# Fewer and wider constant matmuls, one filter couple moved to VectorE, and the last pair's loads and reflections reordered

## The chip, the core and the metric

The kernel runs on one core of one Trainium2 chip. The metric is the device time of an execution in microseconds, lower is better. Engines carry the profile's names: PE (matmuls) and PEld (its weight loads), DVE (VectorE), ACT (ScalarE), POOL (GpSimd) and SP (SyncE, which only issues DMAs here).

## The reference

Two operations follow each other. The first is a causal long convolution along the sequence, done by FFT at double length. The second transforms its output along the sequence, mixes the lowest 64 modes with complex 128 x 128 weights, adds the inverse transform, and ends in a rectified linear layer.

```
x: (8, 5696, 128)   h: (5696, 128)   L = 2 * 5696
x1 = irfft(rfft(x, n=L, axis=1) * rfft(h, n=L, axis=0), n=L, axis=1)[:, :5696]
X = rfft(x1, axis=1)
Y = 0;  Y[:, :64] = einsum('bmd,mde->bme', X[:, :64], w_r + i w_i)
u = x1 + irfft(Y, n=5696, axis=1)
out = u + max(u @ w_ch, 0)          (float32)
```

## The kernel before

All transforms are matmuls with constant matrices in fp16. The sequence is cut as 5696 = 89 x 64. The frequencies of the first cut are k = 0 to 89 (`NK` = 90) and are taken four at a time, which makes 23 ticks (`NT`). The eight batches go in four pairs (`NP`).

The stages, in order:

1. **Start.** `idle(WARM, 6)` issues 52 matmuls of constants into two unused PSUM banks. They compute nothing that is read. Meanwhile h, the constant matrix `M` and the first pair's x (eight pieces `Xr`) are loaded by POOL's queue, and DVE and ACT copy h into the padded tile `Hp`.
2. **h transform.** 64 matmuls make `Ah` from `Hp`.
3. **Filter stage.** Twelve filter couples (`filter_couple`), each for two ticks: 32 matmuls of 64 columns (8 in the last couple) into one of three pairs of PSUM banks, then one cast to `Hs`. Couples 1 and 3 are cast by DVE, the others by ACT. After each couple stand two constant matmuls. After couple 4 is recorded, DVE gets two copies inside `M` (`m_cross`) and then the eight copies `x_place` of `Xr` into the padded tile `Xin`. Four constant matmuls end the stage. SP copies pieces of `Hs` between the halves of the partitions; these copies also wait for the last piece of `Xr`.
4. **a_tiles.** 32 tiles of four matmuls each make `As` from `Xin`. Every a_tile reads all of `Xin`. ACT and DVE share the casts. Then come four constant matmuls.
5. **Ticks of a pair.** `second` (matmuls with `M`), `products` (the multiplication with `Hs` on DVE, after an ACT copy in three ticks of four), `third` (matmuls with `Wc`, cast by ACT, stored to `zscr` by SP), and `modes_of` (matmuls with `G` that collect the 64 modes in PSUM). The next pair's x is loaded and placed meanwhile. At the end of pairs 0 to 2 the next pair's a_tiles follow, and four constant matmuls behind them.
6. **After the last pair.** Two casts give the modes `XT`, the second of them on DVE; `mix` multiplies the modes with the weights `W`, eight transposes and two casts give `C`. The first Z products (`u_z`, tiles `ZT` loaded back from `zscr`, matrix `S4`) are interleaved by hand.
7. **Output.** Z products and `C` products (matrix `IBs`) make `UT`, and a last matmul, a rectifier on ACT and a sum on DVE make the output.

`S4` and `IBs` are loaded only in their first half. The second half is that half reversed and multiplied by a sign per row (`reflect`: DVE for `S4a` and `IBs`, ACT for `S4b`).

The order on every engine is that in which the source records the instructions; nothing is rescheduled. The recorder derives the semaphores from readers and writers of named tokens; an engine stops at the first instruction whose tokens are not there. In the last pair the loads for the output stage are spread over ticks by the table `early`; each entry's loads and clears wait for that tick's product (`pace`). `ZT0`, `ZT1` and so on are five buffers in two parts, of 128 rows (a) and of 52 rows (b) with a cleared margin (`clear_zt`, a memset on POOL); they lie over `As`, `Hs` and `M`, and so each can be loaded only when the ticks that read what lies there are done.

Of the kernel before, what the change touches and what calls it, by code (L numbers as in the profile page):

```python
# [4 lines left out]
P = 128  # L5
# [118 lines left out]
def bass_long_conv_fft__then__afno_spectral_mix_kernel(nc, x, h, moe_w_r, moe_w_i, moe_w_ch, out):  # L124
# [7 lines left out]
    NK = NQ + 1  # L132
    NP = B // 2
# [27 lines left out]
    RB, PB = 2 * NK - P, 32  # L161
# [130 lines left out]
    def ap(t, row, p0, n, off, dims):  # L292
        return bass.AP(t, p0 * row + off, [[row, n]] + [list(d) for d in dims])
# [5 lines left out]
    def pv(bank, off, dims, p0=0, n=P):  # L299
        return bass.AP(ps, p0 * 4096 + bank * 512 + off, [[4096, n]] + [list(d) for d in dims])  # L300
# [10 lines left out]
    def evac(dst, src, reads, writes, scale=None, eng=None, after=()):  # L311
        e = eng
        if e is None:
            turn[0] ^= 1
            e = "scalar" if turn[0] else "vector"
        if e == "scalar":
            if scale is None:
                R.add(e, lambda h_: h_.copy(dst, src), reads, writes, after=after)  # L318
            else:
                R.add(e, lambda h_: h_.activation(dst, src, COPY, scale=scale), reads, writes, after=after)  # L320
        elif scale is None:
            R.add(e, lambda h_: h_.tensor_copy(dst, src), reads, writes, after=after)  # L322
        else:
            R.add(e, lambda h_: h_.tensor_scalar_mul(dst, src, scale), reads, writes, after=after)  # L324
# [4 lines left out]
    def mm(o, l, r, st, sp, reads, writes):  # L329
        R.add("tensor", lambda h_: h_.matmul(o, l, r, start=st, stop=sp), reads, writes)  # L330
# [11 lines left out]
    def turns(name, items):  # L342
        i = ring2.get(name, 0)
        ring2[name] = i + 1
        return items[i % len(items)]
# [24 lines left out]
    def x_place(i, src, toks):  # L370
        R.add("vector", lambda e: e.tensor_copy(bass.AP(x_sb, i * XN * XE, [[XW, NQ], [XE, XN], [XQ, 4], [1, XD]]),
                                                bass.AP(src, 0, [[XB, NQ], [D, XN], [XD, 4], [1, XD]])),
              list(toks) + XZ, [("xin", i)])
# [40 lines left out]
    XSLOT = [0, 2]  # L414
    ZBANK = [4, 5, 6]
    MB = 7
    WARM = 52


    def idle(n, b0, m=P):  # L420
        for i in range(n):
            mm(pv(b0 + i % 2, 0, [[2 * NK, 2], [1, 2 * NK]], 0, m), f1_sb[:, 0:m], ap(f1_sb, 2 * NK, 0, P, 0, [[0, 2], [1, 2 * NK]]),
               True, True, [("f1",)], [bank(b0 + i % 2)])

    idle(WARM, 6)
# [54 lines left out]
    def filter_couple(c_, sl, eng):  # L480
        ks = [k for t in (2 * c_, 2 * c_ + 1) if t < NT for k in ticks[t]]
        n = len(ks)
        for i, k in enumerate(ks):
            for r in range(2):
                for c in range(2):
                    mm(pv(sl + c, i * H2, [[1, H2]]), ap(m_sb, MW, J * c, J, m_col(c, k, r), [[1, P]]),
                       ap(ah_sb, HW, J * c, J, (2 * k + r) * H2, [[1, H2]]), r == 0, r == 1,
                       AHT + mtok(k, c) + [("ag", k)], [bank(sl + c)])
        lo, t1 = ks[0] * D, min(2 * c_ + 1, NT - 1)
        hi = lo + n * D  # L490
        evac(bass.AP(h_sb, lo, [[2 * HW, P], [H2, 2], [D, n], [1, H2]]), pv(sl, 0, [[512, 2], [H2, n], [1, H2]]), [bank(sl), bank(sl + 1)],
             [("h", t, 0) for t in range(2 * c_, t1 + 1)], eng=eng)
        if t1 in HEND:
            g0 = ([-1] + HEND)[HEND.index(t1)] + 1
            lo = KT * g0 * D
            for p0, p1 in ((0, J), (J, 0)):
                dma("sync", h_sb[p0:p0 + J, HW + lo:HW + hi], h_sb[p1:p1 + J, lo:hi], "s", XR[-1] + [("h", i, 0) for i in range(g0, t1 + 1)],
                    [("h", i, 1, p0) for i in range(g0, t1 + 1)])
# [22 lines left out]
    ZX = [("zs", i, b) for i in range(NZ, NZL) for b in range(2)]  # L521
    zt_old = [(AST, AST), (AST, AST), (H_ALL, H_ALL), (H_ALL, H_ALL), (M_ALL[6:12], G_ALL)]

    def load_zt(i, eng="sync", more=()):
        g_, c_ = divmod(i, J // ZB)
        for part, (p0, r0, n) in enumerate(((0, 0, P), (PB, P, RB))):
            old = list(once(("zt", i % NC, part), zt_old[i % NC][part])) + list(more) + pace
            dma(eng, bass.AP(zt[i % NC][part], p0 * ZP, [[ZP, n], [1, ZP]]),
                bass.AP(zs, (g_ * 2 * NK + r0) * J * 256 + c_ * ZB * 256, [[J * 256, n], [1, ZP]]),
                "q" if eng == "gpsimd" else "t", [("zd", g_, s_) for s_ in range(NT)], [("zt", i % NC, part)], after=old)  # L530

    def clear_zt(i):
        z32 = zt[i][1][0:PB, :].bitcast(U32)
        R.add("gpsimd", lambda e: e.memset(z32, 0), (), [("zt0", i)], after=list(zt_old[i][1]) + pace)

    def load_ib():
        dma("gpsimd", ib_sb[:, 0:SH], c_ib.ap(), "p", (), [("ib", 0)], after=M_ALL[0:4] + pace)
# [10 lines left out]
    def load_s4(part):  # L548
        n = PB + RB if part else P
        dma("gpsimd", s4_sb[part][0:n, 0:SH], bass.AP(c_s4, part * SH, [[2 * SH, n], [1, SH]]), "p", (),  # L550
            [("s4", part, 0)], after=pace + (AST if part else M_ALL[2:8]))

    V, A = "vector", "scalar"
    early = {0: lambda: (load_w(6), load_w(7), load_id()),
             6: lambda: load_s4(1), 8: lambda: load_ib(), 10: lambda: load_zt(2, "gpsimd"), 11: lambda: clear_zt(2),
             14: lambda: clear_zt(0), 15: lambda: load_zt(0, "gpsimd"), 16: lambda: load_s4(0),
             NT - 2: lambda: (load_zt(1, "gpsimd", SLACK), clear_zt(1))}
    w_at = {11: (0, 1), 17: (2, 3), 25: (4, 5)}
    pace = []
# [128 lines left out]
    SLOTS = [0, 2, 4, 6]  # L688
    NH = (NT + 1) // 2
    for c_ in range(NH):  # L690
        filter_couple(c_, turns("f", SLOTS[0:3]), "vector" if c_ in (1, 3) else "scalar")
        idle(2, 6)
        if c_ == 4:
            m_cross(4, "vector")
            m_cross(5, "vector")
            for i in range(2 * XC):
                x_place(i, x_raw[i], XR[i])
    idle(4, 6)
    load.update(scalar=0.0, vector=0.0)
    for j in range(32):  # L700
        a_tile(j, [turns("s", SLOTS)], "both" if j == 31 else share(720))
    idle(4, turns("s", SLOTS))
    for g_ in range(NP):
        for t in range(NT + LM if g_ + 1 == NP else NT):
            if g_ == 0 and t % 2 == 0 and t // 2 < NG:
                load_g(t // 2)
            tick(g_, t)
            assert g_ + 1 < NP or not wp
            if g_ == NP - 1 and t in early:
                pace[:] = [("u", min(t, NT - 1) % NU)] if t else []  # L710
                early[t]()
        if g_ + 1 < NP:
            load.update(scalar=600.0, vector=0.0)
            third(g_, NT - 2)
            a_tile(0, [0], share(720))
            a_tile(1, [2], share(720))
            third(g_, NT - 1)
            load["scalar"] += 560.0
            a_tile(2, [0], share(720))
            modes_of(g_, NT - 3)  # L720
            a_tile(3, [4], share(720))
            modes_of(g_, NT - 2)
            a_tile(4, [2], share(720))
            modes_of(g_, NT - 1)
            load["scalar"] += 700.0
        evac(bass.AP(xt, 6 * g_ + 2, [[B * XTW, P], [3 * B, M], [2, 2], [1, 2]]), pv(MB, 0, [[1, M], [M, 2], [P, 2]]),
             [bank(MB)], [("xt", g_)], 1.0 / 64, eng="scalar", after=[("ag", k) for k in range(NS + 2 * XN, NK)])
        evac(bass.AP(xt, 6 * g_, [[B * XTW, P], [3 * B, M], [1, 2]]), pv(MB, M, [[1, M], [P, 2]]),
             [bank(MB)], [("xtn", g_)], -1.0 / 64, eng="vector" if g_ + 1 == NP else "scalar", after=[("ag", k) for k in range(NS + 2 * XN, NK)])
        if g_ + 1 < NP:  # L730
            for j in range(5, 32):
                a_tile(j, [(0, 4, 6, 2)[(j - 5) % 4]], "both" if j == 31 else share(720))
                if j == 31:
                    idle(4, 2)
                if wp and j % 2 == 1:
                    dst, src_, ring, tok = wp.pop(0)
                    dma("gpsimd", dst, src_, ring, (), [tok], after=[("as", j)])
                if g_ + 2 == NP:
                    for i in w_at.get(j, ()):
                        load_w(i)  # L740
# [54 lines left out]
             src, [bank(t), bank(t + 1)], [("u_", ub, 2 * c_ + half)], eng=e, after=once(("u", ub), old))  # L795

    XTT = [(n, g_) for g_ in range(NP) for n in ("xt", "xtn")]
    reflect("vector", s4_sb[0], P, 0, ("s4", 0), M_ALL[2:8])
    reflect("scalar", s4_sb[1], PB + RB, 1, ("s4", 1), AST)
    MQ = M // 4  # L800

# [25 lines left out]
    for hb in range(2):  # L827
        evac(c_sb[:, hb * 512:hb * 512 + 512], ps16[:, (6 + hb) * 1024:(6 + hb) * 1024 + 512], [bank(6 + hb)],
             [("c", hb)], 2.0 * 64 / S, eng="vector" if hb else "scalar", after=WT)
    reflect("vector", ib_sb, P, 2, ("ib",), M_ALL[0:6])  # L830


    n_o = [0]
# [101 lines left out]
```

## Time and profile before

| | us |
|---|---|
| median of 3 runs | 378.26 (377.53 to 379.01) |
| the profiled execution | 377.14 |
| its span, first to last instruction | 375.3 |

Mean granted clock of the profiled execution: 0.998 of full speed.

The stages in the trace, in us from the start of the span:

| stage | from | to |
|---|---|---|
| constants at the start | 2.5 | 13.4 |
| h transform | 13.5 | 20.9 |
| filter stage | 20.9 | 35.8 |
| a_tiles of the first pair | 35.8 | 49.3 |
| last pair's ticks | 212.4 | 253.1 |
| mode products, `C` | 253.1 | 260.5 |
| output | 260.5 | 375.3 |

In the lines of the timeline the columns are: start, length, engine, source line, operation, output <- input, number of instructions that are merged in the line, and in brackets the engine's idle time before it and what ended that. In the chain of waits they are: start, length, and the engine or transfer that the chain runs through. Line 330 is the helper that issues every matmul, line 327 the one that issues every DMA, and lines 318 to 324 are the casts of `evac`; so the tiles tell the stages apart. The tile `F` is `f1_sb`: a matmul `ps<-F` is one of the constants.

### The profile page before, as it was taken

Reading aid. Unit: us, or ns where it says so; the run is one execution under the profiler, and the core shown is the slowest. Engines: PE = TensorE matmul, PEld = TensorE weight load, DVE = VectorE, ACT = ScalarE, POOL = GpSimd, SP = SyncE. Lnnn points to the kernel's source line nnn. Section 1 sums busy time; section 2 is a strip of 40 time slices with the busy share of each in tenths; the row PEclk is TensorE's granted clock in tenths of the full one; section 3 lists DMA queues with packets and bytes.
Section 4 is the critical chain, followed back from the end, with each engine's and each line's share of the span. In section 5 each row is a group of like instructions: output and inputs, shape, how many; then the busy total and the mean of one; then the engine's idle time right before and its main releaser. Section 6 shows DMA issues by size and latency. Waiting matters only on the chain.

```text
span 375.3 us, 12160 instructions
## 1 busy us (share of the span) xinstructions
PE 354.7 (95%) x5208; PEld 267.0 (71%) x5208; DVE 300.7 (80%) x333; ACT 313.4 (84%) x494; POOL 92.0 (25%) x138
## 2 busy tenths in 40 slices
PE   7987989999989999999999899999999999999992
PEld 3755856667856667766667666668898988888871
DVE  7675998998989998889998888764357776787784
ACT  8766989998989998999998899995466777777783
POOL 8760012320923311822213403427000000000000
PEclk9999999999999999999999999999999999999999
DMA  8995939998999996999998989999999999999767
GB/s 140 314 210 132 231 97 239 275 267 244 108 137 220 257 264 170 138 146 228 219 247 193 294 303 294 312 351 372 393 392 391 392 414 416 407 402 359 303 272 298
DMA packets 84129, 101.71 MB, mean 271 GB/s; under 512 B 22078, under 2 KB 68926, under 8 KB 81106
## 3 DMA queue, kind: packets, MB, share of 16 engines
q1 hardware_dynamic: 59643, 67.73, 53.0%
q0 software_dynamic: 24432, 33.20, 43.3%
q8 instruction: 41, 0.67, 0.7%
q14 instruction: 13, 0.11, 0.1%
HBM read 68.38 MB, written 51.12 MB: 318 GB/s over the span
## 4 chain that ended last, share of the span: by engine, by line
PE 79%; ACT 10%; DVE 5%; DMA 3%; issue 2%; DVEq 0%; POOL 0%; POOLq 0%
PE ps L330 79%; ACT As L320 7%; DMA Hin<-in_h_dram 3%; DVE As L324 2%; ACT R L869 1%; DVE U L616 1%; ACT UT L318 1%; ACT Hp L440 1%; DVE Ah L324 0%; DVE UT L322 0%; ACT Ah L320 0%; ACT XT L320 0%; DVE O L870 0%; DVE Os L870 0%; DVEq L105 0%
## 5 line engine op out<-in xcount | busy, mean ns | idle before, releaser
L330 PE MATMUL ps<-U,Wc 128*128 128x512 f16 (+1 forms) x368 | 94.4, 376 | 0.0
L624 DVE TENSOR_TENSOR U<-Xs,Hs 128x2048 f16<-128x2048 f16 (+1 forms) x68 | 80.6, 1188 | 10.9 <-ACT Xs L318 8.8
L318 ACT CAST Xs<-ps 128x1024 f16<-128x1024 f32 (+1 forms) x72 | 69.5, 971 | 7.1 <-PE ps L330 4.9
L870 DVE TENSOR_TENSOR O<-ps,R 128x512 f32<-128x512 f32 x81 | 52.5, 685 | 19.6 <-ACT R L869 12.3
L318 ACT CAST Zs<-ps 128x512 f16<-128x512 f32 (+1 forms) x120 | 62.9, 603 | 0.0
L869 ACT ACTIVATE R<-ps 128x512 f32<-128x512 f32 x96 | 50.9, 572 | 14.3 <-PE ps L330 13.9
L324 DVE TENSOR_SCALAR As<-ps 128x720 f16<-128x720 f32 (+1 forms) x63 | 51.9, 879 | 8.1 <-PE ps L330 7.0
L330 PE MATMUL ps<-As,M 64*128 64x128 f16 x1440 | 48.7, 217 | 4.6 <-DVE U L616 3.5
L330 PE MATMUL ps<-F,Xin 128*128 128x180 f16 x512 | 51.5, 247 | 1.5 <-DVE As L324 0.8
L320 ACT ACTIVATE As<-ps 128x720 f16<-128x720 f32 (+1 forms) x69 | 48.6, 765 | 5.0 <-PE ps L330 4.2
L330 PE MATMUL ps<-WI,UT 128*128 128x256 f16 x360 | 51.8, 279 | 0.5 <-DVE O L870 0.4
L330 PEld LDWEIGHTS ps<-F,Xin 128*128 128x128 f16 x512 | 43.2, 141 | 9.6 <-DVE As L324 5.0
L330 PEld LDWEIGHTS ps<-U,Wc 128*128 128x128 f16 x368 | 28.2, 97 | 28.9 <-ACT Zs L318 6.0
L330 PEld LDWEIGHTS ps<-As,M 64*128 64x128 f16 x1440 | 40.3, 94 | 11.2 <-DVE U L616 4.2
L327 POOL DMA_DIRECT2D Xt<-in_x_dram x48 | 24.8, 520 | 89.6 <-PE ps L330 89.0
L624 DVE TENSOR_TENSOR U<-ps,Hs 128x2048 f16<-128x2048 f32 x20 | 45.7, 2284 | 0.0
L318 ACT CAST UT<-ps 128x712 f16<-128x712 f32 x40 | 30.0, 752 | 16.7 <-PE ps L330 15.8
L330 PEld LDWEIGHTS ps<-WI,UT 128*128 128x128 f16 x360 | 39.3, 152 | 4.2 <-issue 1.9
L330 PE MATMUL ps<-IBs,C 128*128 128x356 f16 x128 | 39.2, 314 | 0.8
L330 PEld LDWEIGHTS ps<-G,Zs 128*128 128x128 f16 x468 | 25.7, 96 | 12.0
L318 ACT CAST Zt<-ps 128x512 f16<-128x512 f32 (+1 forms) x64 | 33.8, 604 | 0.1
L330 PE MATMUL ps<-G,Zs 128*128 128x2 f16 (+2 forms) x468 | 28.8, 191 | 0.0
(91 smaller groups left out, 495.4 us busy)
## 6 DMA issues: line engine op xcount, KB each, us to landing
out_dram<-O SPq DMA_DIRECT2D x39, 512.0 KB, 7.4
zscr<-Zs SPq DMA_DIRECT2D x57, 256.0 KB, 6.9
zscr<-Zt SPq DMA_DIRECT2D x31, 256.0 KB, 7.6
Xt<-in_x_dram POOLq DMA_DIRECT2D x24, 320.0 KB, 6.8
W<-wscr POOLq DMA_DIRECT2D x8, 512.0 KB, 10.4
ZT0a<-zscr SPq DMA_DIRECT2D x3, 1024.0 KB, 9.6
Xr<-in_x_dram POOLq DMA_DIRECT2D x8, 320.0 KB, 17.5
M<-cM POOLq DMA_DIRECT2D x3, 720.0 KB, 12.5
```

The costliest lines, as they stand in the source:

```text
L318: R.add(e, lambda h_: h_.copy(dst, src), reads, writes, after=after)
L320: R.add(e, lambda h_: h_.activation(dst, src, COPY, scale=scale), reads, writes, after=after)
L324: R.add(e, lambda h_: h_.tensor_scalar_mul(dst, src, scale), reads, writes, after=after)
L327: R.add(eng, lambda h_: h_.dma_start(dst, src), reads, writes, ring=ring, after=after)
L330: R.add("tensor", lambda h_: h_.matmul(o, l, r, start=st, stop=sp), reads, writes)
L440: R.add("scalar", lambda e, dst=dst, src=src: e.copy(dst, src), HT, [("hp", c_)])
L616: R.add("vector", lambda e, b=b, s_=s_: e.tensor_tensor(bass.AP(u_s[i], b * 512, [[2048, P], [1024, 2], [1, n * D]]), s_, hv, MULT), [tok, ...
L624: R.add("vector", lambda e: e.tensor_tensor(uv, src, hv, MULT), bk + [("h", t, 0), ("h", t, 1, 0), ("h", t, 1, J)], [("u", i)])
L869: R.add("scalar", lambda e: e.activation(rv, src_r, RELU), bk, [("r", i % NR)], after=once(("r", i % NR), G_ALL + XTT + [("y", q) for q in ...
L870: R.add("vector", lambda e: e.tensor_tensor(ov, src_u, rv, ADD), bk + [("r", i % NR)], [key + (h_,)], after=once(key, old))
```

## The change

- `idle` issues matmuls of 512 columns instead of 360. At the start 37 instead of 52; after each filter couple one instead of two; at the end of the filter stage two instead of four; after the a_tiles of each pair three instead of four. In all 63 instead of 96.
- Filter couple 9 is cast by DVE instead of ACT. It stands in DVE's queue between the seventh and the eighth `x_place`; the eighth is recorded after the loop over the couples.
- In the last pair `ZT2` and `ZT0` are loaded in two parts each, at ticks 9 and 12 and at ticks 10 and 14 instead of at 10 and at 15; `ZT2`'s clear moves from tick 11 to 10.
- The reflections of `IBs` and `S4a` on DVE stand ahead of the casts to `XT` of the last pair, instead of behind them and behind the casts to `C`.

```diff
-    WARM = 52
-    def idle(n, b0, m=P):
+    WARM = 37
+    def idle(n, b0):
         for i in range(n):
-            mm(pv(b0 + i % 2, 0, [[2 * NK, 2], [1, 2 * NK]], 0, m), f1_sb[:, 0:m], ap(f1_sb, 2 * NK, 0, P, 0, [[0, 2], [1, 2 * NK]]),
+            mm(pv(b0 + i % 2, 0, [[1, 512]]), f1_sb[:, 0:P], ap(f1_sb, 2 * NK, 0, P, 0, [[0, 4], [1, P]]),
                True, True, [("f1",)], [bank(b0 + i % 2)])
...
-    def load_zt(i, eng="sync", more=()):
+    def load_zt(i, eng="sync", more=(), parts=(0, 1)):
         g_, c_ = divmod(i, J // ZB)
-        for part, (p0, r0, n) in enumerate(((0, 0, P), (PB, P, RB))):
+        for part in parts:
+            p0, r0, n = ((0, 0, P), (PB, P, RB))[part]
...
-             6: lambda: load_s4(1), 8: lambda: load_ib(), 10: lambda: load_zt(2, "gpsimd"), 11: lambda: clear_zt(2),
-             14: lambda: clear_zt(0), 15: lambda: load_zt(0, "gpsimd"), 16: lambda: load_s4(0),
+             6: lambda: load_s4(1), 8: lambda: load_ib(), 9: lambda: load_zt(2, "gpsimd", (), (0,)),
+             10: lambda: (clear_zt(2), load_zt(0, "gpsimd", (), (0,))), 12: lambda: load_zt(2, "gpsimd", (), (1,)),
+             14: lambda: (clear_zt(0), load_zt(0, "gpsimd", (), (1,))), 16: lambda: load_s4(0),
...
-        filter_couple(c_, turns("f", SLOTS[0:3]), "vector" if c_ in (1, 3) else "scalar")
-        idle(2, 6)
+        filter_couple(c_, turns("f", SLOTS[0:3]), "vector" if c_ in (1, 3, 9) else "scalar")
+        idle(1, 6)
         if c_ == 4:
             m_cross(4, "vector")
             m_cross(5, "vector")
-            for i in range(2 * XC):
+            for i in range(2 * XC - 1):
                 x_place(i, x_raw[i], XR[i])
-    idle(4, 6)
+    x_place(2 * XC - 1, x_raw[-1], XR[-1])
+    idle(2, 6)
...
-    idle(4, turns("s", SLOTS))
+    idle(3, turns("s", SLOTS))
...
+        if g_ + 1 == NP:
+            reflect("vector", ib_sb, P, 2, ("ib",), M_ALL[0:6])
+            reflect("vector", s4_sb[0], P, 0, ("s4", 0), M_ALL[2:8])
         evac(bass.AP(xt, 6 * g_ + 2, ...            (the two casts to XT)
...
-                    idle(4, 2)
+                    idle(3, 2)
...
-    reflect("vector", s4_sb[0], P, 0, ("s4", 0), M_ALL[2:8])
...
-    reflect("vector", ib_sb, P, 2, ("ib",), M_ALL[0:6])
```

## The prediction

> **What bounds the kernel now.** I read the page first (busy shares, DMA queues), then the chain of waits in order of time, then the timeline of the stages that the change touches. The profiled execution took 377.14 us, 1.84 more than its span.
>
> ```profile
> span 375.3 us, 12160 instructions
> PE 354.7 (95%) x5208; PEld 267.0 (71%) x5208; DVE 300.7 (80%) x333; ACT 313.4 (84%) x494; POOL 92.0 (25%) x138
> q8 instruction: 41, 0.67, 0.7%
> ```
>
> PE has work almost throughout, so a gain must come from a place where PE stands still or does needless work on the path. The constant matmuls that the change shortens lie mostly in the first 50 us. The chain there:
>
> ```profile
> 20.89 6.54 PE ps L330 x235
> 27.43 1.51 issue
> 28.94 4.01 PE ps L330 x128
> 32.96 1.08 issue
> 34.04 13.83 PE ps L330 x149
> ```
>
> Two pauses stand in it that no engine or transfer ends ("issue"), 1.51 and 1.08 us, and between them lie exactly 128 matmuls. A matmul has a weight load, so that is 256 instructions. PE has 5208 of each, 10416 instructions, and the instruction queue moved 41 packets: one packet to about 254 instructions, 0.67 MB / 41 = 16 KB each. I read the pauses as PE at the end of an instruction block whose successor has not arrived, at a time when the loads of x fill the DMA queues. From one pause's end to the next it takes 34.04 - 28.94 = 5.10 us. So while these loads run, a block costs about 5.1 us, however fast PE eats its 128 matmuls.
>
> The rest of the filter stage (start us, duration, engine, line, operation):
>
> ```profile
> 23.84 0.64 PE L330 MATMUL ps<-Ah,M 64*128 64x64 f16 x32
> 24.41 0.48 PE L330 MATMUL ps<-F 128*128 128x360 f16 x2
> 24.52 1.23 DVE L322 CAST Hs<-ps 128x1024 f16<-128x1024 f32 x1 [0.74 <-PE ps L330]
> 24.82 0.64 PE L330 MATMUL ps<-Ah,M 64*128 64x64 f16 x32
> ...
> 27.65 4.38 DVE L371 COPY Xin<-Xr 89x2048 f16<-89x2048 f16 x7
> ...
> 29.18 3.97 ACT L318 CAST Hs<-ps 128x1024 f16<-128x1024 f32 x4 [1.68 <-PE ps L330]
> ...
> 33.20 0.69 DVE L371 COPY Xin<-Xr 89x2048 f16<-89x2048 f16 x1 [1.17 <-DMA Xr<-in_x_dram]
> ...
> 34.92 1.09 PE L330 MATMUL ps<-F 128*128 128x360 f16 x6
> ```
> ```profile
> 35.85 12.51 PE L330 MATMUL ps<-F,Xin 128*128 128x180 f16 x128
> ```
>
> The first a_tile needs all eight x_place copies. The last of them ends at 33.20 + 0.69 = 33.89, but PE begins its first a_tile only at 35.85, because it still has couples 10 and 11 and six constant matmuls to do after the second pause. These 1.96 us are what is to be had here.
>
> **Filter stage.** A couple takes 24.82 - 23.84 = 0.98 us: 0.57 for 32 matmuls, then 0.41 for two constants. Six constants took 1.09 us; with 0.32 for the last one's full duration (row below), they start (1.09 - 0.32) / 5 = 0.155 apart, and 512 columns at that rate make 0.22. One such in place of two saves 0.09: a couple takes 0.89, unless a block is late.
>
> Where the blocks end moves. Ahead of the pause at 27.43 PE has had 52 + 64 + 6 x 34 + 31 = 351 matmuls. With 37 at the start and 33 per couple, matmul 352 is the 20th of couple 7 (37 + 64 + 7 x 33 = 332), and the next block begins 128 on, at the fifth matmul of the a_tiles. The block before was entered at couple 3's sixth matmul, 23.94; now it is at couple 3's 24th, 20.89 + 3 x 0.89 + 0.41 = 23.97. So the block arrives as before, at about 29.0, but PE is a couple further on when it stops (27.5). After it: 13 matmuls (0.23) and the constant (0.22 + 0.10 to the next couple) to 29.55, couples 8 to 11 at 29.55, 30.44, 31.33, 32.22, and with the last eight matmuls and three constants PE is ready at 33.1. The next block, 5.10 us after 29.0, is there at 34.1.
>
> The DVE queue: its seven copies end at 32.03 or up to 0.27 earlier (couple 3 is done 3 x 0.09 earlier). Couple 9 is ready at 30.44 + 0.57 = 31.0; its cast, 1.23 as in the row, runs to 33.0 to 33.26. The last copy is queued behind it and waits for its x piece until 33.20 anyway, so it ends at 33.89 to 33.95, and PE starts 0.05 later. ACT without couple 9 casts at 0.99 each (3.97 / 4): couple 10 is out by 32.9, so ACT is free. The fifth a_tile matmul wants its block at 34.3; 34.1 does. First a_tile at 34.0 instead of 35.85: **-1.85 us**. Bounds: -2.1 if the x piece lands earlier (cast end 33.0 + 0.69 + 0.05 = 33.75); -0.4 if the pauses keep their places (a rival). What follows moves with it; the a_tiles are held by ACT and DVE as before.
>
> In a sentence apart: the Trainium skill's page "Runtime: NRT & Kernel Launch", section "Instruction fetch mechanics", says that instructions come in blocks of 16 KiB, 256 each, and that fetching is hidden by the pace of issue; the first agrees with 0.67 MB in 41 packets, the second not with 1.51 and 1.08 us, and by it these pauses would be something else and stay behind the same matmuls, the second rival.
>
> **Start.** The first load of Hp's weights, and the constants ahead of it, 19 in 2.4 to 8.1 us and 33 in 8.5 to 13.3:
>
> ```profile
> 13.46 1.80 PEld L330 LDWEIGHTS ps<-F,Hp 128*128 128x128 f16 x20 [0.44 <-DVE Hp L442]
> ```
> ```profile
> L330 PE MATMUL ps<-F 128*128 128x360 f16 x19 | 5.9, 506 | 2.5 <-DMA F<-cF 2.5
> ```
> ```profile
> L330 PE MATMUL ps<-F 128*128 128x360 f16 x33 | 5.2, 317 | 0.0
> ```
>
> PE speeds up at about 8 us, by time and not by count. 52 x 360 = 18,720 columns become 37 x 512 = 18,944, 0.1 us more at 0.155 per 360. PE now waits 0.44 for the copy of Hp and will wait a little less. **0**; bounds 0 and +0.1, the latter where PE speeds up later than here.
>
> **Ends of the first three pairs and after the first a_tiles.**
>
> ```profile
> 48.20 0.77 PE L330 MATMUL ps<-F 128*128 128x360 f16 x4
> ...
> 49.30 1.07 PE L330 MATMUL ps<-As,M 64*128 64x128 f16 x32 [0.33 <-DVE As L324]
> ```
>
> Four constants (0.62) become three (0.66) in a gap that a DVE cast ends 0.33 after them: **0**, four times; uncovered it would be +0.04 each. Would fewer constants lower the clock? The granted clock at the end of the run, where PE has no matmul at all (the second and third columns after the length are PE and its weight loads; the clock stands third from last):
>
> ```profile
> 370.00:373.00 3.00, 0.00 (x0) 0.00 (x0) 0.25 (x2) 0.00 (x0) 0.00 (x0) 1.00 0.98 371
> 373.00:375.30 2.30, 0.00 (x0) 0.00 (x0) 0.00 (x0) 0.00 (x0) 0.00 (x0) 0.60 0.05 17
> ```
>
> It holds through 3 us of silence. My longest gap is 29.0 - 27.5 = 1.5 us, as long as the present 1.51. **0**.
>
> **Last pair.** Rows of POOL, DVE and PE:
>
> ```profile
> 242.13 0.54 POOL L327 DMA_DIRECT2D S4a<-cS  x1
> ```
> ```profile
> 250.63 0.69 DVE L624 TENSOR_TENSOR U<-Xs,Hs 128x1024 f16<-128x1024 f16 x1 [0.24 <-ACT Xs L318]
> 253.88 0.29 DVE L324 TENSOR_SCALAR XT<-ps 128x128 f16<-128x128 f32 x1 [2.55 <-ACT XT L320]
> 254.09 0.93 DVE L546 TENSOR_SCALAR S4a<-S4a,SG 128x2759 f16<-128x2759 f16 x1
> ...
> 260.48 1.07 DVE L546 TENSOR_SCALAR IBs<-IBs,SG 128x2759 f16<-128x2759 f16 x1
> ```
> ```profile
> 254.27 1.09 PE L330 MATMUL ps<-XT,W 128*128 128x64 f16 x32
> ...
> 256.81 2.03 PE L330 MATMUL ps<-XT,W 128*128 128x64 f16 x64
> ```
> ```profile
> S4a<-cS POOLq DMA_DIRECT2D x1, 734.2 KB, 10.3
> ```
>
> Z parts: POOL issues the ZT2 and ZT0 parts some ticks earlier. Its order becomes ZT2a, clear, ZT0a, ZT2b, clear, ZT0b, S4a; behind them stand only the loads of tick 21 and later. The S4a load, still tied to tick 16, goes out no later than 242.13, and without ZT0a right ahead of it. PE never waited for these loads in this stretch: **0**.
>
> Reflections: DVE is idle from 251.32 to 253.88. IBs (1.07) and S4a (0.93) fit there, to 253.3, and the XT cast behind them, on which PE's mode products wait, has 0.55 to spare. S4a must be there by about 252.4: at its present 10.3 us from issue it lands at 252.43. What leaves 254.09 and 260.48 delayed nothing on the chain. **0**; bounds -0.1 and +0.3 (a POOL memset beside them on SBUF; none runs beside S4a's now).
>
> Blocks in the mode products: 33 matmuls fewer shift the block ends by 33 there. Counting on in 128s, less the other instructions in PE's queue (an estimate), a block begins now near 252.2 and the next near 257.2, 5 us and no pause; shifted, near 254.3 and 258.2, a stretch of 64-column matmuls only 3.9 us long, against 5.10 in the filter stage. PE waits for XT just before, so its queue will have read ahead. Bounds 0 and +1.2; I take **+0.2**, near the present block's no pause.
>
> Sum: -1.85 + 0.2 = **-1.65 us**: 377.14 becomes 375.5. The median of the runs, 378.26 (377.53 to 379.01), stands 1.12 above the profiled execution; set on it, the forecast is 376.6.
>
> **Rivals.**
> - The pause moves into the mode products: nearly the whole +1.2 falls due, -0.75 in all, 377.5. For it: 3.9 us against 5.10. Against: read-ahead.
> - The pauses stay behind the same matmuls. The constants alone then save 12 x 0.09 + 0.18 = 1.26, or, if each pause ends at its old time, only the 0.36 behind the second; middle 0.8, 377.5. Against: exactly 128 matmuls.
> - The start is not PE's: x lands about 2 us later in most runs than in this profile, and the gain is gone: 378.3. For: the last copy is already waiting for it by 1.17.
> - Slower: the S4a reflection, now ahead of the XT cast, waits for its load and holds DVE. From a landing after 253.0 each us costs one; from 254.6 the gain is used up. A landing half as late again as now (15 us after 242.1, 257.1) costs 4.1, net +2.4, 380.7. Against: ZT0a no longer stands right ahead of it, and even 10.3 would do.
>
> **How the numbers follow.** My forecast has 0.58, the rivals in order 0.13, 0.12, 0.11 and 0.06. The forecast's own range is 376.1 to 377.4: -2.1 us, or -0.9 with half of the block's bound and a little of the pauses'. The runs themselves scatter by 0.75 to each side. So 375.4 to 378.4, which takes in the first three rivals. Half a per cent, 1.9 us, is about what a measurement of this kernel can tell from no change; the gain lies just short of it. Over 0.5% faster (below 376.4): 0.34, the better half of my case; within: 0.60, the rest and three rivals; slower: 0.06.
>
> **What would show it.** Right: first a_tile matmul at about 34.0, 0.05 after the last x_place; one pause of about 1.5 us, inside couple 7; no pause with couple 10; mode products as long as now; DVE's two L546 rows between 251 and 254 minus 1.85. Wrong: a_tiles still start after 35; a new "issue" among the XT,W matmuls; an XT cast that waits for S4a; a granted clock under 1 before 370.

## The result, and the profile after

| | before | changed |
|---|---|---|
| median, us (22 runs each) | 377.42 (374.88 to 380.84) | 381.17 (379.12 to 384.35) |
| profiled execution, us | 377.14 | 379.70 |
| its span, us | 375.3 | 377.9 |
| its mean granted clock | 0.998 | 0.989 |

The change makes the kernel slower: ratio 1.0108, 95% interval 1.0089 to 1.0128, some 4 us. The forecast was 376.6 us, in a range from 375.4 to 378.4. The mean granted clock of the 22 changed runs lies between 0.981 and 0.994.

The page of the changed kernel: 66 instructions fewer on PE, nearly the same busy times.

```profile
span 377.9 us, 12091 instructions
PE 355.4 (94%) x5175; PEld 265.0 (70%) x5175; DVE 301.9 (80%) x334; ACT 312.1 (83%) x493; POOL 92.2 (24%) x138
```

The chain of waits tells where the time went (start us, us, what):

```profile
24.12 0.05 issue
24.17 3.72 PE ps L330 x128
27.89 2.20 issue
...
252.59 4.14 PE ps L330 x129
256.72 2.06 issue
258.78 0.95 PE ps L330 x23
```

One pause of note is left in the filter stage, 2.20 us, where there were two; the one that stood in couple 10 is gone. A new pause of 2.06 us stands in the mode products, where there was none. The timeline of the filter stage's end (the last copy and the first a_tile, which begins 0.16 after it), and of the mode products:

```profile
33.44 0.68 DVE L371 COPY Xin<-Xr 89x2048 f16<-89x2048 f16 x1
...
34.28 12.52 PE L330 MATMUL ps<-F,Xin 128*128 128x180 f16 x128
```
```profile
258.78 0.61 PE L330 MATMUL ps<-XT,W 128*128 128x64 f16 x15 [2.06 <-issue]
261.09 2.26 PE L330 MATMUL ps<-IBs,C 128*128 128x356 f16 x7
263.74 0.50 PE L330 MATMUL ps<-IBs,C 128*128 128x356 f16 x1
```

The same two `IBs` lines before the change:

```profile
260.54 1.24 PE L330 MATMUL ps<-IBs,C 128*128 128x356 f16 x7
...
261.95 0.32 PE L330 MATMUL ps<-IBs,C 128*128 128x356 f16 x1
```

Seven matmuls took 1.24 us and take 2.26. The windows around it show why (PE's busy time is the second column, the clock the third from last):

```profile
257.30:260.70 3.40, 1.69 (x37) 1.58 (x38) 0.44 (x2) 0.26 (x1) 2.47 (x3) 1.00 1.09 396
260.70:264.10 3.40, 3.40 (x24) 2.04 (x22) 1.31 (x2) 1.74 (x3) 0.00 (x0) 0.50 0.92 383
```

After 3.4 us in which PE was busy for half, the clock is at 0.50 for the next 3.4 us. The same stretch before the change had PE busy for 3.07 of 3.40 and kept its clock.

So the balance of the two profiled executions reads along the spans: PE begins the a_tiles 1.57 us earlier (34.28 against 35.85); the first `IBs` matmul comes 0.55 later (261.09 against 260.54), which makes 2.1 lost in the mode products; by the eighth it is 1.79 (263.74 against 261.95), and the end is 2.6 later. The last 0.8 falls behind that, partly at a pause of 0.30 at 327.36 in the output stage; I did not take it apart. The median has moved by more than these two executions, 3.75 against 2.56, since the changed kernel's profiled execution is one of its better ones.

### The profile page after: what moved, and what is told of

Same layout as the page of the kernel before. It is cut to its first block, busy times and chain, and to the rows that moved or that the text cites. A ratio compares the mean times of both kernels' runs of the same rounds, so it can differ in the third digit from the quotient of the medians.

```text
span 377.9 us, 12091 instructions
## 1 busy us (share of the span) xinstructions
PE 355.4 (94%) x5175; PEld 265.0 (70%) x5175; DVE 301.9 (80%) x334; ACT 312.1 (83%) x493; POOL 92.2 (24%) x138
## 4 chain that ended last, share of the span: by engine, by line
PE 76%; ACT 10%; DVE 5%; DMA 4%; issue 2%; DVEq 0%; POOL 0%; SPq 0%; POOLq 0%
PE ps L330 76%; ACT As L320 7%; DMA Hin<-in_h_dram 3%; DVE As L324 2%; DMA Hs<-Hs 2%; DVE U L618 1%; ACT R L873 1%; ACT UT L318 1%; ACT Hp L440 1%; DVE Ah L324 0%; DVE UT L322 0%; ACT Ah L320 0%; ACT XT L320 0%; DVE O L874 0%; DVE Os L874 0%
## 5 line engine op out<-in xcount | busy, mean ns | idle before, releaser
L330 PE MATMUL ps<-IBs,C 128*128 128x356 f16 x128 | 40.4, 326 | 0.8
L322 DVE CAST UT<-ps 128x712 f16<-128x712 f32 x24 | 21.4, 891 | 10.9 <-PE ps L330 10.9
```

## The experiments

Kernel 1 is the kernel of experiment 1, kernel 2 that of experiment 2, and so on. Theory 1 after seeing this: 33 matmuls fewer moved the end of an instruction block into the mode products; PE pauses there for the next block, and the clock falls for it. The rival: the moved loads and reflections of the last pair make the pause. Ratios are against the kernel before.

### 1. The missing matmuls put back in the gaps

```diff
-    idle(3, turns("s", SLOTS))            # and idle(3, 2) at the ends of three pairs
+    idle(11, turns("s", SLOTS), 140)      # 11 constants of 140 columns, four times
```

> The changed kernel with 11 constants of 140 columns instead of 3 of 512 in each of the four gaps behind the a_tiles: the same columns (1,540 and 1,536), 32 matmuls more ahead of the mode products. Theory 1 (33 matmuls fewer moved an instruction block's end into the mode products; the pause there let PE's clock fall): block ends in the mode products stand again as before the change, no pause over 0.5 us among the XT,W matmuls, granted clock 1.00 from 250 to 290 us, the gain of the filter stage (1.6 us) is left: about 1.6 us faster than before. Rival (the moved Z loads or reflections of the last pair make the pause, through the DMA queues or DVE): the pause of 2 us and the fall of the clock stay, about 3.7 us slower than before.

Measured: ratio 1.0003 (0.9971 to 1.0035), median 377.03. The mode products have no pause:

```profile
253.75 4.92 PE ps L330 x152
```

The clock is 1.00 from 250 to 290. The columns on PE are the same, so it is the number of instructions and not the work that costs the 4 us. But the gain of 1.6 us did not come. The filter stage of this execution:

```profile
27.48 2.46 issue
```
```profile
26.70:30.10 3.40, 0.94 (x38) 0.60 (x33) 3.37 (x6) 1.16 (x2) 0.00 (x0) 1.00 0.90 178
30.10:33.50 3.40, 3.40 (x80) 2.18 (x73) 1.50 (x4) 2.02 (x2) 0.00 (x0) 0.50 0.34 71
```

Here the clock falls behind the pause of the filter stage, and the first a_tile starts at 35.49, not 34.28.

### 2 and 3. The last pair's edits taken out, and alone

The second kernel is the changed one with the two reflections and the entries of `early` as before the change; the third is the kernel before with only those edits.

> The changed kernel with the last pair's Z loads and reflections as they were before the change; constants and couple 9 as changed. Theory 1: the block's end stays in the mode products, so pause and fallen clock stay, 3 to 4 us slower than before. Rival (Z loads or reflections make the pause): pause gone, 1.6 us faster than before.

> The kernel before with only the last pair's Z loads and reflections changed. Theory 1: within 0.3 us of before, no pause among the XT,W matmuls. Rival (Z loads or reflections make the pause): 3 to 4 us slower than before.

Without the edits the kernel is slow, 1.0163 (1.0113 to 1.0212, from four runs); with them alone it is like before, 0.9986 (0.9957 to 1.0016). That rules the rival out. The chain of the kernel without them:

```profile
24.02 2.21 issue
26.23 3.72 PE ps L330 x128
29.95 2.20 issue
...
260.11 1.68 issue
```

The pause in the mode products is there, and a second one in the filter stage, at 24.02, 128 matmuls before the known one. It was only just avoided in the profile of the changed kernel, 0.05 us at 24.12. First a_tile here: 37.60. In the third kernel, whose filter stage is that of the kernel before, the first a_tile starts at 34.82, 1.03 earlier than in the kernel before: so far apart are two executions of the same filter stage.

### 4. The kernel before with 31 matmuls fewer

```diff
-    idle(WARM, 6)                       # 52 of 360 columns
+    (37 matmuls of 512 columns)
-    idle(4, ...)                        # behind the a_tiles, four times
```

> The kernel before, with 37 constants of 512 columns at the start and none in the four gaps behind the a_tiles: 31 matmuls fewer ahead of the mode products, filter stage and last pair otherwise as before. Theory 1: the pause of about 2 us appears among the XT,W matmuls and the clock falls after it, 2.5 to 3.5 us slower than before (less the 0.6 us by which one block end moves in the filter stage). Rival (Z loads or reflections): no pause, 0 to 0.6 us faster than before. A second rival for the clock (missing constants in the gaps let it fall there): granted clock under 1.00 within 5 us of a pair's a_tiles.

Measured: ratio 1.0119 (1.0080 to 1.0157). Nothing else of the change is in it.

```profile
258.81 2.10 issue
```
```profile
259.00:262.40 3.40, 1.27 (x30) 1.15 (x30) 0.43 (x1) 0.00 (x0) 2.27 (x2) 1.00 1.11 403
262.40:265.90 3.50, 3.50 (x29) 2.48 (x28) 2.09 (x3) 1.64 (x3) 0.00 (x0) 0.51 0.93 380
```

Pause and fallen clock appear, so the block's place is enough to make both. The gaps without constants did not lower the clock at the a_tiles. It fell in the filter stage too, behind a pause of 1.96 us at 24.23.

### 8, 7 and 9. What the block waits for

```diff
# 8: half of the way back
+    idle(7, ..., 180)                   # in place of idle(3, ...)
# 7: loads of the weights, ZT3 and ZT4 wait for the third mode cast
+        load_zt(i, "gpsimd", [("y", 2)])
# 9: load of ZT1, and those behind it, wait for the first mode cast
+            load_zt(1, "gpsimd", SLACK + [("y", 0)])
```

> The changed kernel with 7 constants of 180 columns instead of 3 of 512 in the four gaps: 16 matmuls more ahead of the mode products, half of the way back. The block that now lasts 3.95 us on PE lasts about 4.5 there. Theory 1: a pause of about half, 0.7 to 1.5 us, among the XT,W matmuls. If it were all or nothing: 0 or 2 us.

> The changed kernel with the loads of ZT3, ZT4 and the last weights held back until the third mode cast (about 2.6 us later, behind the pause). If these loads keep the instruction packet waiting in the DMA queues, the pause among the XT,W matmuls shrinks from 2.06 to under 1.2 us. If the packet's time does not hang on them (the loads of ZT1 and the last stores of Z, or a fixed time), it stays at 1.8 to 2.3.

> The changed kernel with the load of ZT1 (and, behind it in POOL's queue, the weights, ZT3 and ZT4) held back until the first mode cast, some 5 us later. If the instruction packet waits behind ZT1's load in the DMA queues (in the runs so far it starts within 1.3 us of its request where ZT1 has only just been issued, and 7 to 8 us after ZT1's issue where the request falls later): packet within 2 us of its request, no pause over 0.5 us among the XT,W matmuls, although the block ends stand as in the changed kernel; PE waits for ZT1 later instead, 1 to 3 us at the first products of ZT1. If the packet waits for something else (the last stores of Z, a fixed time): a pause of 2 us or more as in the changed kernel.

Half of the way back did not halve the pause: 3.79 us in the profile, ratio 1.0071 (1.0030 to 1.0113). So the length is not set by how short a block's stretch is on PE alone, and theory 1 lacked what else sets it. Holding back ZT3 and ZT4 did not help either: the pause was 3.30, ZT3 was issued only after it, and the ratio was 1.0119 (two runs). Its chain:

```profile
258.43 3.30 issue
...
264.25 0.53 POOL ZT3a L327
```

Holding back ZT1 (and the loads behind it) did, although the block ends stand as in the changed kernel (POOL's issue, then the mode products, then the DMA queues from 254.2 to 255.5):

```profile
256.76 0.54 POOL L327 DMA_DIRECT2D ZT1a<-zscr  x1 [14.57 <-PE ps L330]
```
```profile
256.50 2.03 PE L330 MATMUL ps<-XT,W 128*128 128x64 f16 x64
```
```profile
q1 hardware_dynamic: 289, 0.14, 36.8%
q8 instruction: 1, 0.02, 6.7%
```

All 64 products run through. The packet of q8, the queue that I take for PE's instructions, comes in this stretch, in which no load of POOL's queue (q0) is under way. In the changed kernel POOL issues ZT1a at 249.30. Its queues from 252.6 to 256.5, and then from 256.5 to 257.6 (packets, MB, share of the 16 engines):

```profile
q0 software_dynamic: 175, 1.07, 69.0%
q1 hardware_dynamic: 694, 0.35, 29.8%
q14 instruction: 2, 0.02, 1.0%
```
```profile
q1 hardware_dynamic: 475, 0.23, 80.3%
q0 software_dynamic: 86, 0.11, 34.9%
q8 instruction: 1, 0.02, 5.6%
```

First come 1.07 MB of q0 and no packet of q8 (two of q14, another instruction queue), then the packet. So I read it as waiting behind ZT1's load. In the kernel before, ZT1a is issued at 250.91, later against the block's request, and the instruction packet is in the queues between 253.4 and 254.7, in time.

The other profiles bear this reading out. Counted 128 matmuls back from the block's end, PE enters the block ahead at 252.61 in the changed kernel, 3.31 us behind ZT1a's issue, and at 251.84 in the kernel before, 0.93 behind it. In the kernels without a pause there (before, 1, 3, 5, 6, 10) ZT1a is issued 0.20 to 0.93 us ahead of the entry, in kernels 9 and 11 only behind it, and the packet starts 0.91 to 1.87 us after the entry. In the kernels with one (changed, 2, 4, 7, 8) ZT1a is issued 1.39 to 3.31 us ahead, and the packet starts 3.53 to 5.78 us after the entry. Kernel 12 lies between: 1.14 us ahead, 3.22 us, and no pause. What sets the length within these ranges stays open.

PE pays for the late ZT1 in kernel 9 elsewhere, with a wait of 4.04 us for ZT4b that ends at 280.74; as a whole this kernel is slower (ratio 1.021, two runs).

### 5 and 6. The start

The padded kernel's other loss lies in the filter stage. Kernels 1, 2, 7, 8 and 9 have the changed kernel's filter stage, instruction for instruction; their first a_tiles start at 35.49, 37.60, 36.04, 35.52 and 35.70, and only the changed kernel's own profile has 34.28. In all five the clock falls in this stage, in the changed kernel's profile it does not.

The block that is late at 24 us in some of them is, by the reading above, requested when PE passes matmul 96, 352 less twice 128; with 37 constants at the start instead of 52 that is late in the h transform.

```diff
-    WARM = 37        # of 512 columns
+    WARM = 52        # of 364 columns; gaps: 7 of 220      (the fifth kernel)
+    WARM = 42        # of 452 columns; gaps: 10 of 154     (the sixth)
```

> As the first padded kernel (mode products' block ends where they were before the change), but the constants at the start are 52 of 364 columns instead of 37 of 512: the same columns (18,928 and 18,944) and 15 instructions pairs more, so the block end in the h transform lies at 17.6 us again instead of 19.2. Gaps behind the a_tiles: 7 of 220 columns each. Theory A (the later block end is what eats the filter stage's gain in most runs: one more pause at 24 us, and the clock falling after the longer pauses): no pause at 24, pauses in couple 7 (to about 29) and couple 11 (to about 34), first a_tile at 35.0, 0.9 us faster than before and 0.9 us faster than the first padded kernel in the median. Theory B (the halved constants between the couples let the clock fall, wherever the blocks end): granted clock falls after the pause as often as in the first padded kernel, no gain on before.

> As the one with 52, but 42 constants of 452 columns at the start and 10 of 154 in the gaps: the block end in the h transform at 18.7 us, and the third one just behind the filter stage's last matmul. Theory A: no pause at 24 us, one pause in couple 7, first a_tile at 34.2 to 34.4, 1.5 us faster than before. Theory B: the clock falls after the pause in most runs, no gain.

Measured: with 52, ratio 0.9947 (0.9920 to 0.9974), median 375.41; with 42, 0.9963 (0.9931 to 0.9995), median 376.12. The chain and the windows of the one with 52:

```profile
27.25 1.46 issue
28.70 3.59 PE ps L330 x128
32.29 0.41 issue
```
```profile
26.70:30.10 3.40, 1.95 (x71) 1.28 (x66) 3.37 (x6) 1.93 (x3) 0.00 (x0) 1.00 0.92 180
30.10:33.50 3.40, 2.99 (x84) 1.84 (x79) 3.18 (x5) 2.54 (x4) 0.00 (x0) 1.00 0.32 67
```

The pause is an us shorter than in the first padded kernel, PE is busy for 1.95 of 3.4 and not 0.94, and the clock stays. The first a_tile starts at 33.59. So the count of the constants at the start matters. Theory A holds in part only: the padded kernel's own profile has no pause at 24 us, and the kernel with 42, which has none either, but a pause of 2.19 behind which the clock fell, was expected to be the better of the two and is not. What the count changes in the profiles is the pause ahead of the 352nd matmul: with 52 at the start it lasts 1.25 to 1.73 us (kernels before, 3, 5, 10, 11 and 12), with 37 or 42 it lasts 2.19 to 2.48 (changed, 1, 2, 6, 7 and 9; kernels 4 and 8 paused a block earlier). Why it grows stays open.

### 10, 11 and 12. What the other edits are worth

Each is the kernel with 52: with couple 9 cast by ACT again; with the last pair as before the change; with both, so that the constants alone are left.

> The padded kernel with 52 constants at the start, couple 9 cast by ACT again. If DVE's cast of couple 9 is part of the gain: ACT casts couples 7 to 11 in one row from 29.2 to 33.7, first a_tile still near 33.6, first As cast some 0.2 us later, 0 to 0.4 us slower than with DVE's cast. If it is what lets PE finish the stage early: first a_tile after 34.5, 1 us slower.

> The padded kernel with 52 constants at the start, the last pair's Z loads and reflections as before the change. If they are worth nothing, as forecast: within 0.3 us of the kernel with them. If the earlier Z loads keep the DMA queues clearer at the mode products: slower by 0.5 us or more.

> The constants alone: 52 of 364 columns at the start, one per couple, 7 of 220 in the gaps; couple 9 on ACT, Z loads and reflections as before the change (only the eighth x copy is still recorded behind the couples). If the constants carry the whole gain: 0.5 to 0.6 % faster than before, like the same kernel with the last pair's edits. If the last pair's edits carry part of it (the kernel without them, couple 9 on DVE, was 0.04 % faster only, with an interval that leaves this open): within 0.3 % of before.

Measured: 0.9939 (0.9923 to 0.9955, four runs), 0.9996 (0.9965 to 1.0026) and 0.9961 (0.9932 to 0.9990). Taking couple 9 from DVE again costs nothing that these intervals show. The constants alone are faster than before; whether the last pair's edits add something stays open, for their intervals overlap in both comparisons. The kernel with 52 constants, couple 9 on ACT and the new last pair is faster than both given kernels, 0.6% below before (four runs).

## Why the prediction was wrong, step by step

- **Blocks in the mode products: the step that failed.** The shift of the block ends was placed rightly (PE entered the block at 252.6, 254.3 less the gain), and the pause was named as a rival with 0.13. Its size was not: I took the 5.10 us of the filter stage for a block's price and got at most 1.2; it took 6.2 us from 252.59 to 258.78 and paused 2.06. The price is not constant: the packet started 3.92 us after PE entered the block ahead in the changed kernel, 5.78 in kernel 8 and 0.91 in kernel 9, and what was moved in kernel 9 is ZT1's load with those behind it. I chose +0.2 because no pause stood there before, but that showed only that the packet came in time there. The read-ahead that I counted on did not help: PE entered the block at 252.61, only behind its wait for XT.
- **Clock: wrong.** I read from the end of the run that 3 us of silence do no harm. What I had read there was only a fall that had not come yet; the row below it, with 0.60, has the fall. The clock follows stretches of about 3.4 us. The three stretches shown above that end in a fall had PE busy for 0.94, 1.27 and 1.69 us of it. But not every such stretch ends in one. In the changed kernel's filter stage PE was busy for 1.20 of 3.4 us, and the clock stayed:

```profile
26.70:30.10 3.40, 1.20 (x54) 0.80 (x47) 3.36 (x6) 1.56 (x2) 0.00 (x0) 1.00 0.87 171
30.10:33.50 3.40, 3.40 (x119) 2.29 (x121) 3.06 (x6) 2.23 (x3) 0.00 (x0) 1.00 0.23 47
```

  Within one profile the falls begin whole multiples of 3.413 us apart (260.72 and 373.36 in the changed kernel, 33 times), and this grid lies elsewhere in the next execution. I read it so that only the stretches of the grid count: here they are 25.20 to 28.61 and 28.61 to 32.02, and the pause is divided between them. By this reading the same pause lowers the clock in one execution and not in another, and the changed kernel's profile was lucky in its filter stage. How little PE must do in a stretch is not sharp in these runs: the clock fell behind one of kernel 10 with 1.86 us and stayed behind one of kernel 8 with 1.83. The Trainium skill's page "TensorE: Matmul & The Clock Gate", section "What's actually happening", gives a window of 3413 ns and half rate after an idle one; the length agrees with 3.4 us at 0.50 here, but a stretch with PE busy for up to half was enough.
- **Filter stage: right in the one profile, by luck.** -1.85 was forecast, -1.57 came, with one pause in couple 7 as described and none in couple 10. Five other executions of the same filter stage begin the a_tiles at 35.49 to 37.60, against 35.85 and 34.82 in two executions of the stage before (the kernel before and kernel 3): no gain. What I missed is the block before: I only followed the ends that paused in the kernel before, and not the one at matmul 96, which moves from the middle of the h transform to its end. Its successor then comes as late as 26.2 (pauses of 2.21 and 1.96 in kernels 2 and 4); and the pause in couple 7, where it stands, is 2.2 us and more instead of 1.5. With the longer pauses the clock falls there as well. So the term was -1.57 at its best and about 0 or a loss otherwise; with 52 constants and the new couples the first a_tile starts at 33.10 to 34.46 (kernels 5, 10, 11 and 12). The third rival, a late x, is not what took the gain: in kernels 1, 2, 7, 8 and 9 the last copy stands right behind DVE's cast of couple 9, and in kernels 10 and 12, where it does wait for x, it starts at 31.89 and 32.11.
- **Start and gaps: right as far as they went.** The 37 constants took 10.93 us, the 52 took 10.92, and the gaps did not grow. I priced these edits at nothing because time covers them, and it was their instruction count that cost.
- **Reflections and S4a: right.**

```profile
249.55 0.97 DVE L547 TENSOR_SCALAR IBs<-IBs,SG 128x2759 f16<-128x2759 f16 x1
250.44 0.92 DVE L547 TENSOR_SCALAR S4a<-S4a,SG 128x2759 f16<-128x2759 f16 x1
252.19 0.29 DVE L324 TENSOR_SCALAR XT<-ps 128x128 f16<-128x128 f32 x1 [0.83 <-ACT XT L320]
```

  They fit ahead of the XT cast with 0.83 us to spare, and the slower rival that I gave 0.06 did not come. The memset beside them took 2.48 us instead of 1.82, and POOL still issued its next load earlier than before (253.05 against 253.70).
- **The sum.** The sign turned because two terms taken as 0.2 and 0 came to about 2.1 and 1.2. With the gain of 1.57 and the 0.8 that I did not take apart this makes the 2.6 us between the two profiled executions. The medians lie 3.75 apart; that the missing gain of the filter stage makes the rest fits the five other profiles, but is not shown run by run. My range was set by the scatter of the runs and the first three rivals, which were all priced with the clock at 1.

## What to carry to other kernels

On a long unrolled engine program, removing instructions that cost no time is not free of effect: it moves every later block end, and one of them may land where the engine runs short instructions and a big load is already under way (here from 1.4 us after its issue). After such an edit, count where the block ends fall (here every 128 matmuls with their loads) against the bulk loads, and keep the count with short filler instructions in a gap if the places were good. Judge a pause by what it does to the clock too.

## What the runs showed of the hardware that was not expected

- At the mode products a 16 KB instruction packet starts 3.5 to 5.8 us after PE enters the block ahead, if the 1.4 MB load of ZT1 was issued 1.4 us or more before; 0.9 to 1.9 us after, if it was issued within the last 0.93 us or only later.
- The Trainium skill's page "Runtime: NRT & Kernel Launch", section "Instruction fetch mechanics", calls the cost of a block's end mostly hidden. Here it was 2.06 us in one place and 2.20 in another of the same run.
- PE's clock falls to 0.50 for 3.4 us after some stretches of 3.4 us in which PE was busy for about half or less (0.94 to 1.86), and not after others (1.20); the falls of one execution lie on a grid of 3.413 us. One fall cost 1.2 us where matmuls fill PE (1.79 less 0.55 in the changed kernel).
